# HGRN2 attention and low-rank mixer on one core: DMAs of the unused path on ScalarE, a branch hint, four first loads, and four blocks mixed as one piece

## Chip, cores, metric

The kernel runs on one core of a Trainium2 chip. The metric is the time of one launch in microseconds (us) of device time; of several runs the median is given. A profiled execution of the same program gives the trace that all other numbers come from.

## What is computed

```python
f = sigmoid(f_logit)                                  # q, k, v, f_logit: (4, 8, 768, 48)
for t in range(768):
    state = f[:, :, t, :, None] * state + k[:, :, t] (outer) v[:, :, t]
    y[:, :, t] = q[:, :, t] @ state
x = y.transpose(0, 2, 1, 3).reshape(4, 768, 384)
h = (x.transpose(0, 2, 1) @ U) @ V                    # U (768, 32), V (32, 768)
u = x + h.transpose(0, 2, 1)
out = u + relu(u @ w_ch1) @ w_ch2                     # 384 -> 1536 -> 384
```

The weights arrive in float64 and are turned into float32 on the chip; everything else is float32.

## The kernel before

Two paths are in the program. `factored_path` (L538) does the work by blocks of 64 and 128 tokens, with gates kept as sums of logarithms, and also finds out whether the gates allow this: a flag `ok` (L1304, read at L1603). `general_path` (L1309) stands inside `tc.If(good == 0)` (L1604) and computes the same in a way that holds for any gates. For the inputs here the flag is 1 and the general path is jumped over: each engine that has code in it ends with a compare-and-branch (L1604) to a target behind that code. The program's last steps (L1632) are semaphores between the engines.

**Attention.** A unit is one batch and two heads: 16 units, four in a batch. For a unit the logits are loaded by `load` (L603), on SyncE's queue, 128 tokens on the partitions in six blocks. For unit 0 they then go through `logs` in two halves of three blocks: a clamp on VectorE (L775), an exponential and a logarithm on ScalarE (L777, L779), sums over time by products on TensorE (`log_sums`, L790), and exponentials of these (L803 to L808). Keys and queries are multiplied by these, and scores (L926), states (L974), the sums of states (L996, L1000) and outputs (L1012, L1030) follow; the scans over time are on VectorE (L827, L845). TensorE's order is written out by hand for the whole kernel (`manual_schedule`); VectorE's, ScalarE's and SyncE's for the first part only. Elsewhere a scheduler orders VectorE and ScalarE, and adds of the mixer go in at high priority (`add`, L201 to L204).

Ahead of all this stands a `blank` tile, 128x384, that is set to zero (L640) and read by warm-up products (`busy`, L1131) while the first loads are under way. After the loads of unit 0's f, k and q come those of the next unit's f and unit 0's v.

**Mixer.** The class at L157 holds the steps for one batch: `low_rank` (L187) and `added_up` (L194) make h for four groups of 32 rows; `mix(t)` (L208) multiplies one 128-token block's slice of V (32 rows, in row group t modulo 4 of the array) with h, 128x384, and after every second block adds both to x in one VectorE instruction of 128x768; `turn` (L253) transposes x into uT; `ch1` (L273) and `ch2` (L324) are the two large products; `seven` (L371) does the second with seven products of half-size blocks where `sums` of weights are at hand, and `fewer` (L422) the first with fifteen products instead of eighteen, from sums of weights and of x. `store` (L318) writes 128 tokens from SyncE.

The mixer of batch b runs piece by piece between the steps of batch b+1's attention (`Fill`). Where a batch's mixing stands:

- Batch 0's is done in parts of columns by `mix_of` (L234) near 41 us; the change doesn't touch it.
- Batches 1 and 2: `start_mixer` (L1112) runs `before`: `low_rank`, `added_up`, all six `mix`, then `turn`, with the last pieces of the batch before (`after`, second products) between them.
- Batch 3, in the last stage, after all attention: the list at L1277 to L1306 puts `low[:2]` and the three pieces of `mixes` (L510; each a pair of blocks) between pieces of `fewer` of another pair of blocks; `of(i, "ready")` are sums of z on VectorE that `seven` needs.

**PSUM.** Tiles come from two pools: `ps_big`, three tiles of two banks (mixing pairs, transposes, products of `fewer`), and `ps_mm`, two tiles of one bank (`low_rank`, `ch1`'s pz, `ch2`'s po, which is filled in four quarters and so is held over other pieces). [...] A tile is given out in turn, and its next writer waits for its last reader.

**DMA.** Eight semaphores are used in turn by all DMAs: each DMA waits for the one eight before it, and at the end SyncE waits for each.

Of the kernel before, what the change touches and what calls it, by code (L numbers as in the profile page):

```python
# [10 lines left out]
F32 = mybir.dt.float32  # L11
# [4 lines left out]
ALU = mybir.AluOpType  # L16
# [43 lines left out]
def weight_loader(nc, pool, dma):  # L60

    P = nc.NUM_PARTITIONS

    def load(dst, w, place=None):
        if w.dtype == F32:  # L70
            return lambda: dma.dma_start(out=dst, in_=w), *[lambda: None] * 3
        rows, n = dst.shape[0], dst.free_size()
        T = {}

        def shaped(t):
            return t if len(dst.shape) == 2 else t.rearrange("p (c n) -> p c n", c=dst.shape[1])


        def start():
            raw = pool.tile([P, WP], U64, name="w_raw", bufs=RAW) if place is None else place()  # L80
            raw = T["raw"] = raw[0:rows, 0:n]
            dma.dma_start(out=shaped(raw), in_=w)

        def halves():
            y = pool.tile([P, WP], U32, name="w_y")[0:rows, 0:n]
            r = pool.tile([P, WP], I32, name="w_r", bufs=3)[0:rows, 0:n]
            words = T["raw"].bitcast(U32).rearrange("p (n two) -> p n two", two=2)
            lo, hi = words[:, :, 0], words[:, :, 1]

            f = y.bitcast(F32)  # L90
            nc.scalar.activation(f, hi.bitcast(F32), AF.Abs)  # L91
            nc.scalar.activation(r, lo, AF.Copy, scale=2.0**-29)
            T["parts"] = y, r, hi

        def join():
            y, r, hi = T["parts"]
            f = y.bitcast(F32)
            nc.vector.tensor_scalar(f, f, SMALLEST, LARGEST, ALU.max, ALU.min)  # L98
            nc.vector.tensor_scalar(y, y, 3, 0x3FFFFFFF, ALU.logical_shift_left, ALU.bitwise_and)
            nc.vector.scalar_tensor_tensor(y, hi, 0xC0000000, y, ALU.bitwise_and, ALU.bitwise_or)  # L100
            nc.gpsimd.tensor_tensor(dst.bitcast(I32), shaped(y.bitcast(I32)), shaped(r), ALU.add)  # L101

        def end():
            halves()
            join()

        return start, end, halves, join

    return load
# [47 lines left out]
class Mixer:  # L157
# [6 lines left out]
    def __init__(self, tc, b, x, U, V, w1, w2, sums, ident, blocks, out, two, three, zp, ps_big, ps_mm, wide=False,  # L164
                 z_all=None, room=None, pair=0):
        nc = tc.nc
# [41 lines left out]
        def mix(t):  # L208

            s = t % 2  # L210
            if s == 0:
                pu[0] = ps_big.tile([P, 2, 512], F32, name="pu", tag="big")
            g = slice((t % NG) * R, (t % NG + 1) * R)
            nc.tensor.matmul(pu[0][:, s, 0:DM], lhsT=V[g, t // NG, :], rhs=h[1][g, :], start=True, stop=True)  # L214
            if s == 1:
                add(x[:, t - 1 : t + 1, :], x[:, t - 1 : t + 1, :], pu[0][:, :, 0:DM], ALU.add)


        hs, last = {}, {}

        def low_rank_of(cols):
# [94 lines left out]
        self.some = low_rank_of, added_up_of, mix_of, turn_of, ch1_of  # L316

        def store(t, o):  # L318
            nc.sync.dma_start(out=out[b, t * P : (t + 1) * P, :], in_=o)

        po = {}
        NQ = 4
# [171 lines left out]
            return [(4 * NDC * 2 * P, lambda j=j: ch1(a, j)) for j in range(NI)]  # L494


        parts = [low_rank, added_up, lambda: [mix(t) for t in range(NCH)]]
        parts += [lambda a=a: turn(a) for a in range(NA)]
        self.before = [(DM, piece) for piece in parts]

# [6 lines left out]
            self.main += ready(a) + ahead[: NI // 2] + halved(a) + ahead[NI // 2 :]  # L507
        self.main += ready(NA - 1)
        self.after = second(NA - 1)
        self.mixes = [(DM, lambda t=t: [mix(t), mix(t + 1)]) for t in range(0, NCH, 2)]  # L510
        self.first, self.second, self.ready, self.fewer, self.halved = first, second, ready, fewer, halved
        self.sums_of_x = lambda a: [(1, lambda: sums_of_x(a))]

# [24 lines left out]
def factored_path(ctx, tc, q, k, v, f_logit, moe_U, moe_V, moe_w_ch1, moe_w_ch2, out, ok):  # L538
# [64 lines left out]
    def load(n, *names):  # L603

        b, hp = divmod(n, HP)
        for nm in names:
            if nm == "v":
                v_tiles[n] = three.tile([P, NBL, 2, D], F32, name="v_nat")
            for par in range(2):
                head = src[nm][b, 2 * hp + par]  # L610
                if nm in "kq" and n < HP:
                    if par == 0:
                        nc.sync.dma_start(
                            out=packed(n, nm).rearrange("p (h t) -> p h t", h=2),
                            in_=src[nm][b, 2 * hp : 2 * hp + 2].rearrange("h (p c) d -> p h (c d)", p=P),
                        )
                    continue
                if nm == "v" and par:

                    for s in range(2):  # L620
                        nc.sync.dma_start(
                            out=v_tiles[n][(1 - s) * C : (2 - s) * C, :, par, :],
                            in_=head.rearrange("(c s p) d -> s p c d", s=2, p=C)[s],
                        )
                    continue
                if nm == "v" or n < TURNED:
                    dst = v_tiles[n] if nm == "v" else nat[n % 2][nm]
                    nc.sync.dma_start(out=dst[:, :, par, 0:D], in_=head.rearrange("(c p) d -> p c d", p=P))
                    continue
                head = head.rearrange("(c i) d -> i c d", i=NB)  # L630
                for part in range(2):
                    p0 = par * PAD + part * NB
                    n_ch = min(NB, D - part * NB)
                    nc.sync.dma_start(  # L634
                        out=raw[n % 2][nm][p0 : p0 + NB, :].rearrange("p (c d) -> p c d", d=NB)[:, :, 0:n_ch],
                        in_=head[:, :, part * NB : part * NB + n_ch],
                    )

    blank = late[:, 5, 0 : 3 * P]
    nc.vector.memset(blank, 0.0)  # L640
    load(0, "f", "k", "q")
    load(1, "f")
    load(0, "v")

# [481 lines left out]
    with tc.manual_schedule(engines={nc.vector.engine, nc.scalar.engine}):  # L1126
# [3 lines left out]

        def busy(n, cols=DM):  # L1131
            for _ in range(n):
                nc.tensor.matmul(idle[:, 0:cols], lhsT=blank[:, 0:P], rhs=blank[:, 0:cols], start=True, stop=True)

        written = ExitStack()
        written.enter_context(tc.manual_schedule(engines={nc.sync.engine}))
# [133 lines left out]
    def of(i, kind):  # L1270
        if i >= len(pairs):
            return []
        b, a = pairs[i]
        return getattr(mixers[b], kind)(a)
# [5 lines left out]
    for i in range(len(pairs)):  # L1280
        ahead, behind = of(i + 1, "fewer"), of(i, "second")
        nxt = of(i + 2, "sums_of_x")
        if not ahead:
            todo += behind
            break
        todo += of(i, "ready")
        if i == 0:
            todo += [p for two_of in zip(ahead, low[:2] + mixers[1].mixes) for p in two_of] + behind[:1] + low[3:4] + nxt
        else:
            todo += (low[4:] if i == 1 else []) + ahead[:4] + nxt + ahead[4:5]  # L1290
            if i + 2 < len(pairs):
                todo += behind[:1]
        if i + 2 < len(pairs):
            todo += ahead[5:6] + behind[1:2] + ahead[6:7] + behind[2:3] + ahead[7:] + behind[3:]
        else:
            todo += ahead[5:6] + behind[:1] + ahead[6:] + behind[1:2] + of(i + 1, "ready") + behind[2:]
# [12 lines left out]
def general_path(ctx, tc, q, k, v, f_logit, moe_U, moe_V, moe_w_ch1, moe_w_ch2, out):  # L1309
# [87 lines left out]
    def load_unit(n):  # L1397
        b, hp = divmod(n, HP)
        for nm in "fkq":
            for par in range(2):  # L1400
                nc.sync.dma_start(
                    out=nat[n % NSLOT][nm][:, :, par, 0:D],
                    in_=src[nm][b, 2 * hp + par].rearrange("(c p) d -> p c d", p=C),
                )
        v_tiles[n] = three.tile([P, NCH, 2, D], F32, name="v_nat")
        for par in range(2):
            nc.sync.dma_start(
                out=v_tiles[n][:, :, par, :],
                in_=src["v"][b, 2 * hp + par].rearrange("(c p) d -> p c d", p=C),
            )  # L1410

    load_weight = weight_loader(nc, two, nc.sync)
    weights = [load_weight(U, moe_U.rearrange("(c p) r -> p c r", p=P))]
    weights += [load_weight(*pair) for pair in by_rows(V, moe_V, R)]
    weights += [
# [165 lines left out]
@with_exitstack  # L1581
def kernel(
    ctx: ExitStack,
    tc: tile.TileContext,
    q: bass.AP,
    k: bass.AP,
    v: bass.AP,
    f_logit: bass.AP,
    moe_U: bass.AP,
    moe_V: bass.AP,  # L1590
    moe_w_ch1: bass.AP,
    moe_w_ch2: bass.AP,
    out: bass.AP,
):


    nc = tc.nc
    args = (q, k, v, f_logit, moe_U, moe_V, moe_w_ch1, moe_w_ch2, out)
    flag = ctx.enter_context(tc.tile_pool(name="flag", bufs=1))
    ok = flag.tile([1, 1], I32, name="ok")  # L1600
    with ExitStack() as inner:
        factored_path(inner, tc, *args, ok)
    good = nc.values_load(ok[0:1, 0:1], min_val=0, max_val=1)  # L1603
    with tc.If(good == 0):  # L1604
        with ExitStack() as inner:
            general_path(inner, tc, *args)

# [29 lines left out]
```

## Time and profile before

| | |
|---|---|
| time, median of 3 runs | 471.83 us (470.58 to 473.95) |
| profiled execution, its own time | 471.81 us |
| its span (first to last instruction) | 470.0 us |
| granted TensorE clock, mean | 0.998 |
| share of the time of 16 DMA engines, 0 to 47 us | 0.80 |
| the same, 161.7 to 276 us | 0.31 |
| chain that ended last, by engine | PE 75%, DVE 13%, issue 3%, ACT 3%, DMA 2%, SyncE's queue 2% |
| costliest group | L279, 492 products 128x256, 111.5 us |

PE is TensorE, PEld its loading of weights (which overlaps PE), DVE VectorE, ACT ScalarE, POOL GpSimd, SP SyncE; a name with q (SPq, DVEq) means that engine's sequencer: register, branch, semaphore and DMA-issuing instructions. A line of a timeline gives start, length, engine, line in the kernel, operation, what it writes and reads, its shape and how many there are in the group; a bracket at the end gives idle time just before it and what ended that. A group's length contains the stops between its members. The chain of waits goes back from the last instruction to what released each one, and lists start, length and what it was. The clock stays at full speed in every slice, so lengths in different stages can be compared.

### The profile page before, as it was taken

Reading aid. Unit: us, or ns where it says so; the run is one execution under the profiler, and the core shown is the slowest. Engines: PE = TensorE matmul, PEld = TensorE weight load, DVE = VectorE, ACT = ScalarE, POOL = GpSimd, SP = SyncE. Lnnn points to the kernel's source line nnn. Section 1 sums busy time; section 2 is a strip of 40 time slices with the busy share of each in tenths; the row PEclk is TensorE's granted clock in tenths of the full one; section 3 lists DMA queues with packets and bytes.
Section 4 is the critical chain, followed back from the end, with each engine's and each line's share of the span. In section 5 each row is a group of like instructions: output and inputs, shape, how many; then the busy total and the mean of one; then the engine's idle time right before and its main releaser. Section 6 shows DMA issues by size and latency. Waiting matters only on the chain.

```text
span 470.0 us, 13005 instructions
## 1 busy us (share of the span) xinstructions
PE 456.2 (97%) x5639; PEld 394.9 (84%) x5639; DVE 352.3 (75%) x579; ACT 165.6 (35%) x315; POOL 54.2 (12%) x60
## 2 busy tenths in 40 slices
PE   7999999999999999999999999999999999999995
PEld 5876888875666578999898878989979999999995
DVE  5767788979999677775675659977796877759632
ACT  5775776562332144322323133232312312112200
POOL 2002445634112001010101001020000000000000
PEclk9999999999999999999999999999999999999999
DMA  9947997577678504506334020000000000000001
GB/s 194 209 107 191 226 220 179 155 116 106 120 120 130 83 18 52 77 7 110 48 66 73 7 52 19 12 3 20 18 1 1 35 1 35 0 16 20 1 36 40
DMA packets 148313, 34.36 MB, mean 73 GB/s; under 512 B 136790, under 2 KB 146710, under 8 KB 148246
## 3 DMA queue, kind: packets, MB, share of 16 engines
q1 hardware_dynamic: 148246, 33.44, 36.4%
q8 instruction: 46, 0.75, 0.7%
q14 instruction: 21, 0.17, 0.1%
HBM read 28.70 MB, written 4.72 MB: 71 GB/s over the span
## 4 chain that ended last, share of the span: by engine, by line
PE 75%; DVE 13%; issue 3%; ACT 3%; DMA 2%; SPq 2%; POOL 0%; DVEq 0%; ACTq 0%; POOLq 0%
PE pw L365 25%; PE pz L279 18%; PE pp L468 12%; PE po L331 5%; PE y L1012 2%; PE y L1030 2%; PE ds L974 1%; PE sc L926 1%; PE pt L744 1%; PE pt L790 1%; SPq L634 1%; PE pu L214 1%; DVE late L845 1%; DMA v_nat<-in_v_dram 1%; DVE kz L721 1%
## 5 line engine op out<-in xcount | busy, mean ns | idle before, releaser
L279 PE MATMUL pz<-uT,w 128*128 128x256 f32 x492 | 111.5, 382 | 0.3
L279 PEld LDWEIGHTS pz<-uT,w 128*128 128x128 f32 x492 | 91.7, 190 | 12.9 <-ACT uT L268 0.6
L1000 POOL COPY st<-added 128x576 f32<-128x576 f32 x12 | 18.2, 1513 | 188.0 <-DVE added L996 188.0
L365 PE MATMUL pw<-zw,w_raw 128*128 128x192 f32 x216 | 38.0, 329 | 0.0
L365 PE MATMUL pw<-w,z_all 128*128 128x192 f32 x216 | 37.3, 327 | 0.0
L101 POOL TENSOR_TENSOR w<-w_y,w_r 128x384 int32<-128x384 int32 x24 | 31.5, 1313 | 39.5 <-DVE w_y L100 23.2
L365 PEld LDWEIGHTS pw<-w,z_all 128*128 128x128 f32 x216 | 35.3, 190 | 0.5
L365 PEld LDWEIGHTS pw<-zw,w_raw 128*128 128x128 f32 x216 | 35.1, 190 | 0.6 <-issue 0.3
L314 ACT ACTIVATE z_all<-pz 128x512 f32<-128x512 f32 x33 | 19.6, 598 | 45.1 <-PE pz L279 44.6
L827 DVE TENSOR_TENSOR_SCAN late<-fz,late 128x768 f32<-128x768 f32 x12 | 21.1, 1756 | 7.3 <-ACT fz L822 7.1
L461 ACT ACTIVATE other<-other 128x512 f32<-128x512 f32 x18 | 11.3, 631 | 40.3 <-DVE other L204 40.3
L331 PE MATMUL po<-w,zw 128*128 128x384 f32 x72 | 25.2, 495 | 0.0
L331 PE MATMUL po<-w,z_all 128*128 128x384 f32 x72 | 24.7, 493 | 0.0
L939 DVE TENSOR_TENSOR A<-sc,causal 128x768 f32<-128x768 f32 x16 | 15.2, 952 | 9.5 <-PE sc L926 9.5
L845 DVE TENSOR_TENSOR_SCAN late<-fz,other 128x768 f32<-128x768 f32 x12 | 22.0, 1834 | 0.2
L331 PEld LDWEIGHTS po<-w,zw 128*128 128x128 f32 x72 | 13.2, 190 | 9.6 <-issue 0.8
L331 PEld LDWEIGHTS po<-w,z_all 128*128 128x128 f32 x72 | 13.3, 190 | 8.9 <-DVE o L204 0.6
L981 ACT COPY added<-ds 48x576 f32<-48x576 f32 (+1 forms) x28 | 17.8, 635 | 5.1 <-PE ds L974 4.7
L461 ACT ACTIVATE z_all<-z_all 128x512 f32<-128x512 f32 x12 | 7.6, 630 | 33.3 <-DVE z_all L204 33.3
L468 PE MATMUL pp<-v_nat,late 128*128 128x128 f32 x152 | 19.1, 275 | 0.0
L1012 PEld LDWEIGHTS y<-st,qT 48*64 48x64 f32 x704 | 13.6, 137 | 6.4 <-issue 3.9
L98 DVE TENSOR_SCALAR w_y<-w_y 128x384 f32<-128x384 f32 (+3 forms) x27 | 12.1, 448 | 8.9 <-ACT w_y L91 8.9
(224 smaller groups left out, 867.3 us busy)
## 6 DMA issues: line engine op xcount, KB each, us to landing
w_raw<-in_moe_w_ch_dram SPq DMA_DIRECT2D x18, 384.0 KB, 4.1
out_dram<-o SPq DMA_DIRECT2D x24, 192.0 KB, 2.0
v_nat<-in_v_dram SPq DMA_DIRECT2D x16, 144.0 KB, 4.3
v_nat<-in_v_dram SPq DMA_DIRECT2D x32, 72.0 KB, 3.9
zw<-in_moe_w_ch_dram SPq DMA_DIRECT2D x6, 384.0 KB, 5.1
w<-in_k_dram SPq DMA_DIRECT2D x4, 288.0 KB, 3.7
w<-in_q_dram SPq DMA_DIRECT2D x4, 288.0 KB, 5.1
late<-in_f_logit_dram SPq DMA_DIRECT2D x10, 96.0 KB, 3.0
```

The costliest lines, as they stand in the source:

```text
L101: nc.gpsimd.tensor_tensor(dst.bitcast(I32), shaped(y.bitcast(I32)), shaped(r), ALU.add)
L279: nc.tensor.matmul(pm[:, i * 2 * P : (i + 1) * 2 * P], lhsT=w1[:, m, o : o + P], rhs=uT[a][:, m, :], start=(m == 0), stop=(m == NDC - 1))
L314: nc.scalar.activation(z[a, c][:, k : k + 2, :].rearrange("p i t -> p (i t)"), pm, AF.Relu)
L331: nc.tensor.matmul(pm, lhsT=z[a, i // NI][:, i % NI, s * P : (s + 1) * P], rhs=w2[:, i, :], start=(i == 0), stop=(i == NFC - 1))
L365: nc.tensor.matmul(W["pm"][:, n * HM : (n + 1) * HM], lhsT=lhs[:, i, :], rhs=rhs[:, i, :], start=(i == 0), stop=(i == NI - 1))
L461: nc.scalar.activation(dst, dst, AF.Relu, scale=float(SIGNS[n]))
L468: nc.tensor.matmul(pm[:, i, r * P : (r + 1) * P], lhsT=room["w"](wn)[:, r * P : (r + 1) * P], rhs=x_node(a, xn), start=((xn, wn) == of[0]) ...
L827: nc.vector.tensor_tensor_scan(backwards(X, S - 1, S), backwards(f, S, S), backwards(ends, S - 1, S), 0.0, ALU.mult, ALU.add,)
L845: nc.vector.tensor_tensor_scan(Y, f[:, 0:S], starts, 0.0, ALU.mult, ALU.add)
L981: nc.scalar.copy(added[r, 1:].rearrange("p (e c s) -> p e c s", c=NBL, s=2), ds[r, :, 0 : NBL * D].rearrange("p s (c e) -> p e c s", e=D),)
L1000: nc.gpsimd.tensor_copy(st, states.rearrange(by_e, c=NCH))
L1012: nc.tensor.matmul(o(c % 2, par, c // 2), lhsT=T["q"][rows[par], chunk[c]], rhs=T["st"][rows[par], c, :], start=(c <= 2), stop=False, skip ...
```

## The change

1. **General path.** Its loads of q, k, v, f and of weights, and its stores, are issued by ScalarE, where SyncE issued them. None of this runs here; it changes how many instructions of each engine lie behind the branch.
2. **Hint.** A hint "likely taken" for VectorE's branch is placed, and the `If` gets the label that it names.
3. **First loads.** Unit 0's f is loaded in four pieces (blocks 0 to 2 of both heads, then blocks 3 to 5), one head on SyncE's queue and one on ScalarE's, where it was two loads of a head each on SyncE's. `blank` becomes 128x1, read with a step of 0.
4. **Mixing.** `mix_four` does blocks 0 to 3 as one piece: four products, blocks 0 and 1 into one `ps_big` tile, 2 and 3 into two `ps_mm` tiles; one add of 128x768 and two of 128x384. Blocks 4 and 5 stay a pair. It is used for batches with `sums` (1 to 3). In the last stage there are two pieces of `mixes` in place of three, and the `ready` sums of the first pair move behind the piece `ahead[4]`.

```diff
+        def mix_product(dst, t):
+            g = slice((t % NG) * R, (t % NG + 1) * R)
+            nc.tensor.matmul(dst, lhsT=V[g, t // NG, :], rhs=h[1][g, :], start=True, stop=True)
+
+        def mix_four():
+            big = ps_big.tile([P, 2, 512], F32, name="pu", tag="big")
+            pms = [big[:, s, :] for s in range(2)] + [ps_mm.tile([P, 512], F32, name="pu1", tag="mm") for _ in range(2)]
+            for t, pm in enumerate(pms):
+                mix_product(pm[:, 0:DM], t)
+            add(x[:, 0:2, :], x[:, 0:2, :], big[:, :, 0:DM], ALU.add)
+            for t in range(2, NG):
+                add(x[:, t, :], x[:, t, :], pms[t][:, 0:DM], ALU.add)
+
+        def mix_blocks():
+            first = 0
+            if sums is not None:
+                mix_four()
+                first = NG
+            for t in range(first, NCH):
+                mix(t)
...
         def store(t, o):
-            nc.sync.dma_start(out=out[b, t * P : (t + 1) * P, :], in_=o)
+            by = nc.scalar if z_all is None else nc.sync
+            by.dma_start(out=out[b, t * P : (t + 1) * P, :], in_=o)
...
-        parts = [low_rank, added_up, lambda: [mix(t) for t in range(NCH)]]
+        parts = [low_rank, added_up, mix_blocks]
...
-        self.mixes = [(DM, lambda t=t: [mix(t), mix(t + 1)]) for t in range(0, NCH, 2)]
+        self.mixes = [(DM, mix_four), (DM, lambda: [mix(t) for t in range(NG, NCH)])]
...
-    blank = late[:, 5, 0 : 3 * P]
+    blank = late[:, 5, 0:1]
     nc.vector.memset(blank, 0.0)
-    load(0, "f", "k", "q")
+    queues = nc.sync, nc.scalar
+    for m in range(2):
+        some = slice(m * NBL // 2, (m + 1) * NBL // 2)
+        for par in range(2):
+            queues[par].dma_start(out=nat[0]["f"][:, some, par, 0:D],
+                                  in_=f_logit[0, par].rearrange("(c p) d -> p c d", p=P)[:, some, :])
+    load(0, "k", "q")
     load(1, "f")
     load(0, "v")
...
-                nc.tensor.matmul(idle[:, 0:cols], lhsT=blank[:, 0:P], rhs=blank[:, 0:cols], start=True, stop=True)
+                nc.tensor.matmul(idle[:, 0:cols], lhsT=blank.broadcast_to((P, P)), rhs=blank.broadcast_to((P, cols)),
+                                 start=True, stop=True)
...
-        todo += of(i, "ready")
         if i == 0:
-            todo += [p for two_of in zip(ahead, low[:2] + mixers[1].mixes) for p in two_of] + behind[:1] + low[3:4] + nxt
+            todo += [p for two_of in zip(ahead, low[:2] + mixers[1].mixes) for p in two_of] + ahead[4:5]
+            todo += of(0, "ready") + behind[:1] + low[3:4] + nxt
         else:
-            todo += (low[4:] if i == 1 else []) + ahead[:4] + nxt + ahead[4:5]
+            todo += of(i, "ready") + (low[4:] if i == 1 else []) + ahead[:4] + nxt + ahead[4:5]
...
-            nc.sync.dma_start(
+            nc.scalar.dma_start(
                     out=nat[n % NSLOT][nm][:, :, par, 0:D],
...
-    load_weight = weight_loader(nc, two, nc.sync)
+    load_weight = weight_loader(nc, two, nc.scalar)
...
+    tc.mark_branch_hint_location("general", "LikelyTaken", engines=[nc.vector.engine])
     good = nc.values_load(ok[0:1, 0:1], min_val=0, max_val=1)
-    with tc.If(good == 0):
+    with tc.If(good == 0, label="general"):
```

More of the change, by code (lines that the diff above doesn't have):

```diff
@@ L1406, in load_unit @@
         for par in range(2):
-            nc.sync.dma_start(
+            nc.scalar.dma_start(
                 out=v_tiles[n][:, :, par, :],
```

## Prediction

> **What bounds the kernel now.** I read the page's first part, then the windows view by stage, then the chain of waits at the start, and the timelines of TensorE and VectorE around the code that changes.
>
> ```profile
> PE 456.2 (97%) x5639; PEld 394.9 (84%) x5639; DVE 352.3 (75%) x579; ACT 165.6 (35%) x315; POOL 54.2 (12%) x60
> ```
> ```profile
> 161.70:276.00 114.30, 114.00 (x1384) 100.44 (x1382) 79.37 (x108) 34.25 (x62) 4.85 (x4) 1.00 0.31 51
> ```
> TensorE is busy 456.2 of 470.0 us. In the second line (stage, length, then busy time of PE, PEld, DVE, ACT, POOL) it lacks only 0.3 us of 114.3. So an edit counts by what it adds to or takes from TensorE's idle time; only the first microseconds, before TensorE has data, and the last ones, after its last product, belong to others. The start, from the chain of waits (start, length, what):
>
> ```profile
> 0.81 0.45 SPq L628
> ...
> 1.32 3.39 DMA late<-in_f_logit_dram
> ...
> 4.81 0.32 DVE late L775
> ...
> 5.16 0.45 ACT late L777
> ...
> 5.63 0.45 ACT late L779
> ...
> 6.17 1.71 PE pt L790 x12
> ```
> The two loads of unit 0's gates, issued at 0.81 and 1.32, take 2.8 and 3.4 us (least and most of "DMA to landing" of these two): landings at about 3.65 and 4.71. The clamp L775 waits for the second.
>
> The mixing of batch 1 (first two lines TensorE's timeline, last two VectorE's):
>
> ```profile
> 160.17 1.56 PE L214 MATMUL pu<-h,V 32*128 32x384 f32 x12
> 161.66 4.14 PE L331 MATMUL po<-w,zw 128*128 128x384 f32 x12
> ```
> ```profile
> 160.18 1.76 DVE L845 TENSOR_TENSOR_SCAN late<-fz,other 128x768 f32<-128x768 f32 x1
> 161.85 2.66 DVE L204 TENSOR_TENSOR x<-x,pu 128x768 f32<-128x768 f32 x3
> ```
> TensorE goes through twelve passes (six blocks) in 1.49 us without a stop, while VectorE is still in a scan. Then batch 2's and the last batch's mixing on TensorE:
>
> ```profile
> 270.70 1.99 PE L214 MATMUL pu<-h,V 32*128 32x384 f32 x12
> 272.67 2.22 PE L365 MATMUL pw<-w,w_raw 128*128 128x192 f32 x12
> ```
> ```profile
> 342.02 0.92 PE L214 MATMUL pu<-h,V 32*128 32x384 f32 x4
> 343.38 1.13 PE L468 MATMUL pp<-st,fz 128*128 128x128 f32 x8 [0.44 <-DVE qT L204]
> 344.34 1.06 PE L468 MATMUL pp<-uT,late 128*128 128x128 f32 x8
> 345.95 0.91 PE L214 MATMUL pu<-h,V 32*128 32x384 f32 x4 [0.55 <-DVE x L204]
> ...
> 348.78 0.91 PE L214 MATMUL pu<-h,V 32*128 32x384 f32 x4
> 349.62 4.17 PE L365 MATMUL pw<-w,other 128*128 128x192 f32 x24
> ```
> And the branch at the end (its instructions by engine, with duration in ns and start):
>
> ```profile
> L1604 SPq EVENT_SEMAPHORE  x8: 17/17/17, 468.1 to 468.6; - x8
> ...
> L1604 DVEq COMPARE_BRANCH  x1: 72/72/72, 465.3 to 465.3; - x1
> L1604 SPq COMPARE_BRANCH  x1: 50/50/50, 465.4 to 465.4; - x1
> ...
> L1604 DVEq EVENT_SEMAPHORE  x1: 21/21/21, 468.5 to 468.5; - x1
> ```
> SyncE jumps at 465.4 and shows its next instruction 2.6 us later; VectorE's jump takes 3.1 us. The last store is issued at 465.03 and lands 2.0 later, at 467.06: both jumps end after it, so they hold the end.
>
> [...]
>
> **The change, part by part.**
>
> *First gate loads.* Four loads of half size on two queues, both halves of blocks 0–2 first: issued near 0.8 on SyncE and ScalarE at once. The bytes are the same and all gate loads finish together near 4.4 to 4.7; the first halves, issued as early as before's first load, should land near its 3.65 or earlier. Then the clamp runs at 3.75 (0.32), exp 4.07 (0.45), log 4.53 (0.45), and TensorE can start at 5.05. The second half follows: clamp end about 5.1, exp 5.5 (ScalarE is busy until then), log end near 6.0. So the L790 products (1.71) end about 6.88, before 7.88: 1.0 us, or 0.7 if the second half lands at 5.0. Two more issues on ScalarE come ahead of its table load (1.28 us), which then ends near 3.2, under the 4.07 where it is needed. SyncE still issues two loads before k and q, and v lands at 9.1 to 10.1 for a need at 10.6. The smaller memset (0.38 to some 0.06 us) starts the warm-up products earlier, so these don't hold TensorE at 5.05. From here the chain has only SyncE waits tied to work that moves along; I take 0.9, ends 0 (the DMA share before 47 us is 0.80, so k, q and v may come no earlier) and 1.1.
>
> *Mixing of batch 1.* Blocks 0 and 1 get a two-bank tile, 2 and 3 a single bank each. At 160 one of the two single banks holds a half-done po (L331). So block 3 must wait until VectorE's add has read block 2, and VectorE comes to this only after the scan (161.85) and the add of blocks 0 and 1 (pitch 0.87): 162.72 + 0.55 for a 128x384 add = 163.27. TensorE then has three products left, 0.84 us (the x4 row at 342.02 took 0.85 to its follower): po starts at 164.17 instead of 161.66, +2.5. Behind the waiting product stands all of TensorE, and for it wait VectorE's o<-x,po (165.83) and the turn into uT on ScalarE. As the stage has 0.3 us of idle time, nothing gives this back. Ends: 0, if the po bank is free there, and 3.5, if the scheduler's order on VectorE puts another piece between.
>
> *Mixing of batch 2.* Here no single bank is held; before, the third pair had to wait for a double one, until VectorE was done with pw (271.63). After, six blocks fit without a wait: 1.49 instead of 1.97, -0.5 (0 to -0.5).
>
> *Mixing of the last batch.* Before, three pairs at 342.02, 345.95, 348.78, each 0.84 for two blocks: the passes of a pair use two row groups of 32. Four blocks fill four row groups and should take the 0.84 of one pair; the third pair's 0.84 goes. The order gives VectorE qT<-A,pp earlier too, since a 0.95 sum (w<-other,w, at 341.68) moves behind: the 0.44 wait and most of the 0.55 go. Added: pp from 342.87, two groups 1.99 to 344.86, pair 4+5 at 345.07 (it waits for the x add, 0.2), pp to 347.89, where pw started at 349.62: -1.7 (ends -0.8, if the four run one after the other, and -1.9). The extra add (two of 0.55 instead of one 0.95) is hidden under VectorE's waits of 1.3 to 1.9 us at 354 to 366; without these it costs 0.15.
>
> *General path.* It isn't run, but its code lies between each branch and its target. In the built program SyncE's share falls from 287 instructions to 1, and ScalarE's rises from 371 to 585. [...]it next waits for the landing at 467.06, not 468.08: -1.0 from SyncE. ScalarE jumps at 455.4, 10 us before the end[...]. VectorE's 652 instructions keep their 3.1 us, and its semaphore at 468.48 gates the program's last steps (0.5 us before what SyncE needs at 469.0)[...]. The hint is one instruction, built in as VectorE's very first. No trace shows one. If it works -1.0 in all; if not -0.5. I take -1.0; ends 0 and -1.0, and +3.1 for the rival below.
>
> Sum: -0.9 + 2.5 - 0.5 - 1.7 - 1.0 = -1.6 on a span of 470.0, so 468.4, and 470.2 with the 1.8 outside it (profiled execution 471.81, median 471.83: no correction).
>
> **Rivals.** (a) *Most gains don't arrive*: the hint does nothing (-0.5 only), and the 0.9 at the start is lost again to the loads of 10 to 47 us. Then -0.5 + 2.5 - 0.5 - 1.7 = -0.2: 471.6. For it: a DMA share of 0.80; against: the first loads of each later step have slack of 2.6 us. (b) *The stall of batch 1 isn't there*, because the scheduler puts the adds ahead of the scan or the bank is free: -4.1, 467.7. Against it: adds wait on TensorE's products at 160.2, just when the scan starts. (c) [...] (the other side): it sits before VectorE's first memset[...]. I price it at VectorE's jump, 3.1 us; its memsets (0.96 to 3.6) would then push the clamp, due at 3.75, past 6. -1.6 + 0.5 + 3.1 = +2.0: 473.8. It decides from 1.6 us on. For it: nothing else stands so early[...].
>
> **How the numbers follow.** Likeliest 0.48: 470.2 (own range 469.0 to 471.3). (a) 0.19, (b) 0.14, (c) 0.14, others 0.05. 80% from 467.5 to 473.4: it takes in (a), most of (b) and the lower part of (c). One per cent, 4.7 us, is about what a measurement can tell from no change. Faster than 467.1 needs (b) and more: 0.05. Slower than 476.5 needs (c) with a second loss: 0.06. The rest 0.89.
>
> **What would show it.** Right: the first clamp near 3.75 and L790 done near 6.9; one gap of 2.3 to 2.5 us on TensorE before the fourth mixing product near 161, released by VectorE's x; none in the mixing near 270; pw in the last stage 1.7 earlier relative to 338; SyncE's first L1604 event with the landing; VectorE's under 0.5 us after its branch. Wrong: a VectorE that starts late, or a gap near 161 that is absent or over 3.5 us.

## The result, and the profile after

The changed kernel takes 472.66 us (median of 22 runs, 469.39 to 475.04), the kernel before beside it 472.45 (22 runs, 470.29 to 474.59): ratio 1.0007, 95% interval 0.999 to 1.0024. The forecast of 470.2 was 0.34% below before; the interval excludes that. The medians of the kernel before differ a little between comparisons (471.75 to 472.47), so ratios count below.

The profiled execution took 475.04 us (span 473.2), the longest of the 22. That turns out to be useful, since it shows two things that I had not counted. In the lines below pu is the tile of the mixing's products, po that of `ch2`, pw that of `seven`, and put that of the transposes into uT. First the page's line of busy time, then the windows view around batch 1's mixing (stage, length, busy PE, PEld, DVE, ACT, POOL, granted clock, DMA share, GB/s):

```profile
PE 459.4 (97%) x5639; PEld 397.2 (84%) x5639; DVE 352.4 (74%) x582; ACT 166.0 (35%) x315; POOL 54.4 (11%) x60
```
```profile
163.70:165.90 2.20, 0.00 (x0) 0.00 (x0) 2.15 (x3) 0.00 (x0) 0.00 (x0) 1.00 0.00 0
167.10:170.40 3.30, 3.30 (x6) 1.67 (x5) 1.17 (x2) 0.00 (x0) 0.00 (x0) 0.50 0.00 0
170.50:174.00 3.50, 3.35 (x44) 2.14 (x42) 1.38 (x2) 0.85 (x2) 0.00 (x0) 1.00 0.00 0
```
TensorE does as many products as before, but is 3.2 us longer busy. It stands still for 2.2 us, and soon after that runs for 3.3 us at a granted clock of 0.50: six passes of po that start 0.64 us apart, where at full clock they start 0.32 apart. That is time that the busy column counts as work.

The stop itself, on TensorE and on VectorE (timelines of the changed kernel):

```profile
162.77 0.92 PE L221 MATMUL pu<-h,V 32*128 32x384 f32 x6
165.91 0.58 PE L221 MATMUL pu<-h,V 32*128 32x384 f32 x1 [2.21 <-DVE x L204]
```
```profile
162.78 1.76 DVE L873 TENSOR_TENSOR_SCAN late<-fz,other 128x768 f32<-128x768 f32 x1
164.46 1.39 DVE L204 TENSOR_TENSOR x<-x,pu 128x768 f32<-128x768 f32 x2
```
Three blocks go through, and the fourth waits for VectorE's adds behind the scan. (The trace names both adds in one row; the second has 128x384.) This is the wait that was forecast.

Batch 2, and the last stage up to pw, on TensorE:

```profile
277.48 0.93 PE L221 MATMUL pu<-h,V 32*128 32x384 f32 x8
278.23 0.81 PE L214 MATMUL pu<-h,V 32*128 32x384 f32 x4
278.96 2.22 PE L387 MATMUL pw<-w,w_raw 128*128 128x192 f32 x12
```
```profile
348.31 0.93 PE L221 MATMUL pu<-h,V 32*128 32x384 f32 x8
...
351.37 0.91 PE L214 MATMUL pu<-h,V 32*128 32x384 f32 x4 [0.15 <-DVE x L204]
...
354.10 2.12 PE L387 MATMUL pw<-w,other 128*128 128x192 f32 x12
```
Eight passes of four blocks take as long as four passes of two did (0.93 against 0.92), and in batch 2 the mixing takes 1.48 us from its first pass to pw, where it took 1.97.

The start, from the chain of waits, and the branch (durations in ns, then starts):

```profile
1.07 4.21 PE idle L1161 x6
...
5.31 2.23 PE pt L818 x12
```
```profile
L1634 SPq EVENT_SEMAPHORE  x8: 17/17/17, 471.3 to 471.8; - x8
...
L1634 DVEq COMPARE_BRANCH  x1: 84/84/84, 469.7 to 469.7; - x1
...
L1634 DVEq EVENT_SEMAPHORE  x1: 21/21/21, 470.3 to 470.3; - x1
```
L818 is L790 of before. It starts 0.86 us earlier, but takes 2.23 us in place of 1.71. At the end VectorE's jump takes 0.6 us, not 3.2, and SyncE's first semaphore (471.30) follows the last store's landing (471.29).

If each TensorE instruction is matched with its twin in the trace of before, the changed kernel lags behind by this much (us; a minus means that it is ahead):

| place | lag |
|---|---|
| end of L790 | -0.33 |
| 31 us, after two stops without a semaphore (before has one there) | +1.57 |
| 37 us, after a first stretch of half clock (34.0 to 37.4) | +2.76 |
| first pass of batch 1's mixing | +2.60 |
| po behind it | +5.10 |
| end of the second stretch of half clock | +6.79 |
| pw after batch 2's mixing | +6.30 |
| pw in the last stage | +4.48 |
| last product | +4.38 |
| end, with 3.84 us after VectorE's last add in place of 4.99 | +3.23 |

### The profile page after: what moved, and what is told of

It is laid out like the page before. It is cut to its first block, busy times and chain, and to the rows that moved or that the text cites. A ratio compares the mean times of both kernels' runs of the same rounds, so it can differ in the third digit from the quotient of the medians.

```text
span 473.2 us, 13013 instructions
## 1 busy us (share of the span) xinstructions
PE 459.4 (97%) x5639; PEld 397.2 (84%) x5639; DVE 352.4 (74%) x582; ACT 166.0 (35%) x315; POOL 54.4 (11%) x60
## 4 chain that ended last, share of the span: by engine, by line
PE 77%; DVE 12%; issue 3%; ACT 3%; DMA 3%; SPq 1%; POOL 0%; DVEq 0%; ACTq 0%; POOLq 0%
PE pw L387 25%; PE pz L300 20%; PE pp L490 12%; PE po L353 4%; PE y L1040 2%; PE y L1058 2%; DMA v_nat<-in_v_dram 2%; PE sc L954 2%; PE pt L772 2%; PE pt L818 1%; PE ds L1002 1%; DVE late L873 1%; DVE late L855 1%; PE pt L981 1%; DVE late L908 1%
## 5 line engine op out<-in xcount | busy, mean ns | idle before, releaser
L353 PE MATMUL po<-w,zw 128*128 128x384 f32 x72 | 26.8, 521 | 0.0
```

The source lines that it names most:

```text
L353: nc.tensor.matmul(pm, lhsT=z[a, i // NI][:, i % NI, s * P : (s + 1) * P], rhs=w2[:, i, :], start=(i == 0), stop=(i == NFC - 1))
```

## Experiments

**One part each, and batch 1 undone.** Four kernels on one chip, with 43 runs of the kernel before (median 471.75).

*pairs_batch1*: the changed kernel, where batch 1 goes without the piece of four.

```diff
-            if sums is not None:
+            if sums is not None and b != 1:
                 mix_four()
```


> The changed kernel, but batch 1's six blocks are mixed as three pairs, as before; batches 2 and 3 keep the piece of four. Theory (stall and clock): in the changed kernel's profiled execution TensorE stood 2.2 us before the fourth product and then had half its clock for 3.4 us (167.1 to 170.5), together 4.0 us from one matched product to the next. Both must be gone: the pu passes in about 1.5 us without a gap, no half clock between 160 and 175, and the median 2 to 4 us below the changed kernel's 472.7, so 469 to 470.5, some 0.5% under the kernel before. Rival (the stall is made up for later): the gap goes, the time stays within 1 us of 472.5.

468.51 us, ratio 0.9931 (0.9917 to 0.9945). The pu passes take 1.49 us without a stop, and none of its six executions is under a mean clock of 0.998. One line of the change costs 3.6 us against the changed kernel (ratios 1.0007 and 0.9931: 0.76%), more than the 2.5 of the wait (+2.60 to +5.10 above). At 0.69% under the kernel before it is also faster than the 0.5% that was expected.

*head_only*: before with the four loads and the small blank; *tail_only*: before with the general path's DMAs moved and the hint; *mix_only*: before with the mixing and its order in the last stage. Each is that part of the diff, alone.

> The kernel before with the four first loads and the 128x1 blank alone. Theory[...]: L790 is done 0.3 to 1.0 us before the 7.98 of the kernel before, 0.3 where the clock becomes full only after 5.5 us; between 20 and 40 us the stops that wait for no semaphore, 0.98 us before and 2.6 after, come at the same instructions, 256 apart, of a length that changes from execution to execution; median within 0.7 us of the kernel before. Rival (as forecast): 0.9 is kept to the end. Rival (the change of the loads itself delays later loads): the lead turns into a loss of over 1 us that waits for a DMA show.

471.99 us, 1.0004 (0.999 to 1.0019). In its profile L790 is done at 7.01, against 7.87 before, yet the median shows no gain.

> The kernel before with the general path's DMAs on ScalarE and the hint alone. Theory: from VectorE's last add to the end 3.8 us instead of 5.0, so 1.2 less, about 471.2; VectorE's jump about 0.5 us instead of 3.1, SyncE's next instruction within 0.05 of the last store's landing. Rival (the hint costs something at the start): TensorE's first products of L790 start later than 6.2, and the gain is less than 0.5. Its head and its mixing are those of the kernel before: its list of clocks shows how often that has a stretch of half clock; theory: rarely, and none at 160 to 175.

470.51 us, 0.9975 (0.9963 to 0.9986): -1.2. From VectorE's last add to the end 3.62 us, where the profile of before has 4.99.

> The kernel before with the mixing of four blocks alone, for batches 1 to 3, and the order of the last stage that goes with it. Theory: +2.2 to +4.0 at batch 1 (the wait, and the half clock where it follows), -0.3 at batch 2, -2.0 in the last stage: 0 to +1.7, so 472.4 to 474. Rival (the wait is hidden): -2.3, 470.1. Rival (last stage gains nothing): +2 to +4.

472.96 us, 1.0032 (1.0012 to 1.0051): +1.5. Its 17 executions fall into groups by mean clock: 472.04 (median of 6, clock 0.997 and more), 474.03 (5, clock 0.994 to 0.996), 475.51 (6, under 0.994). None of the 43 executions of before is under 0.994. The three parts add up to 0.2 - 1.2 + 1.5 = +0.5, about the +0.3 of the whole.

**Is it the stop that brings the half clock?** *stall_warm* keeps the wait and gives TensorE something to do in it:

```diff
             for t, pm in enumerate(pms):
+                if t == 3 and b == 1:
+                    spare = ps_big.tile([P, 2, 512], F32, name="spare", tag="big")
+                    for _ in range(3):
+                        nc.tensor.matmul(spare[:, 0, 0:DM], lhsT=ident, rhs=h[1], start=True, stop=True)
                 mix_product(pm[:, 0:DM], t)
```


> The changed kernel with three extra products (identity by h, 128x384, result unused) between batch 1's third and fourth mixing product, where TensorE stood for 2.2 us. They fill about 1.9 us of it. Theory (the stop costs twice, by itself and by the half clock that follows): po starts where it did, within 0.3 us, but no half clock follows, so executions under a mean clock of 0.994 vanish; median 0.8 to 1.8 us below the changed kernel's 472.66, so about 471.3. Rival (the half clock has another reason, or costs nothing): clocks and time as in the changed kernel, or later by what the extra products take beyond the gap.

471.37 us, 0.9988 (0.9976 to 1.0). TensorE's timeline:

```profile
161.70 2.20 PE L230 MATMUL spare<-h,ident 128*128 128x384 f32 x6
...
164.83 4.14 PE L357 MATMUL po<-w,zw 128*128 128x384 f32 x12
```
po starts 3.98 us after the first pu (160.85), as in the changed kernel (162.77 to 166.76, 3.99), and its twelve passes take the usual 4.14 us. 19 of 22 executions have a mean clock of 0.997 or more, where the changed kernel had 4 of 22; one is under 0.994, where it had 8. Doing useless work in the gap takes 1.3 us off the median. So the half clock is the stop's second price: it goes when the stop is filled, and it goes when the stop is taken away (pairs_batch1).

**The tail in its parts.** *tail_no_hint* has the moved DMAs only, *hint_only* the hint only.

> The kernel before with the general path's DMAs on ScalarE, without the hint. Theory: VectorE's jump takes 3.1 us again and its semaphore comes 3.2 us after its branch, where SyncE waits for it: from VectorE's last add to the end about 4.4 us, 0.5 us less than the 5.0 of the kernel before and 0.6 more than with the hint; median about 471.2. Rival (VectorE's jump doesn't matter): 3.8 us as with the hint.

471.54 us, 0.9988 (0.9972 to 1.0003); tail 4.42 us, as worked out. At the branch's line SyncE is early and VectorE late:

```profile
L1605 SPq EVENT_SEMAPHORE  x8: 17/17/17, 464.7 to 466.1; - x8
...
L1605 DVEq EVENT_SEMAPHORE  x1: 21/21/21, 467.5 to 467.5; - x1
```


> The kernel before with the hint alone; the general path's DMAs stay on SyncE. Theory: VectorE's jump 0.5 us, but SyncE's jump still takes 2.6 us, so from VectorE's last add to the end about 5.0 us as in the kernel before, median within 0.4 of it; TensorE's first products start as in the kernel before, so the hint costs nothing. Rival[...]: L790 starts later than 6.3 us, and the median is 1 to 3 us up.

472.95 us, 1.0016 (1.0 to 1.0032); tail 5.16 us: VectorE is ready 0.6 us after its branch, but SyncE's jump takes 2.83, so the end gains nothing. L790 starts at 5.90, among the profiles with the old loads (5.74 to 6.73), and the hint takes 0.05 us on VectorE, so rival (c) has nothing in the trace. The median is 0.8 us over the kernel before, where at most 0.4 was expected. That lies at the edge of the interval; I can't attribute it.

**The stops without a semaphore.** In the changed kernel TensorE stands twice for over a microsecond near 25 and 30 us without any semaphore to wait for:

```profile
26.82 0.49 PE L1058 MATMUL y<-v_nat,A 64*64 64x48 f32 x18 [1.35 <-issue]
...
29.54 0.92 PE L954 MATMUL sc<-qT,kz 48*64 48x64 f32 x46
31.72 0.27 PE L954 MATMUL sc<-qT,kz 48*64 48x64 f32 x2 [1.26 <-issue]
```
Before them stand 961 and 1217 recorded instructions of TensorE, 256 apart. In all 18 profiles every such stop of over 0.15 us from 12 us on stands behind 705, 961, 1217, 1473 or 1985 of them, always a multiple of 256 apart. The profile's page shows on queue q8 46 transfers of kind "instruction", 0.75 MB, so 16 KB each, beside 11278 product and weight instructions of TensorE, 245 to a transfer. One runs from 24.49 to 25.44 us and one from 29.42 to 30.43, each ending 0.03 us before one of these stops begins (25.47 and 30.46). That such a transfer brings a stretch of TensorE's code is an estimate from these counts, and that the stops have to do with it isn't shown. *shift_blocks* moves the count against the program (on the kernel with batch 1 in pairs):

```diff
-        busy(3)
+        busy(1)
+        busy(8, 16)
```


> The changed kernel with batch 1 mixed in pairs, and a warm-up of one large and eight small products (16 columns) in place of three large ones: TensorE has 24 product and weight instructions more ahead of unit 0. Theory[...]: the stops come after the same number of recorded TensorE instructions as before, about 962 and 1218, so 12 products earlier in the program: in the group y<-v_nat,A after some 16 products and not after 28. Rival (they belong to the data of that product): the same products, 986 and 1242 instructions. The time is not the question; it may be up to 1 us later, since the warm-up ends later and TensorE's clock may be full later.

```profile
29.82 0.79 PE L954 MATMUL sc<-qT,kz 48*64 48x64 f32 x34
32.13 0.46 PE L954 MATMUL sc<-qT,kz 48*64 48x64 f32 x14 [1.52 <-issue]
```
The stop comes again after 1217 instructions, and so twelve passes earlier in the group (34 and 14 in place of 46 and 2). The stops belong to the count of instructions, not to the product's data. (470.51 us, 0.9966, 0.9951 to 0.9982: by the ratios 1.7 us over pairs_batch1. In its profile the clock is full only at 11.2 us, which may be why; it was not tested.)

Whether the stops come from the data traffic was tried by holding two weight loads back (*later_weights*). `elif n == 2:` allots the tile, writes one column of it from x and issues the two loads, which at n == 1 are left out:

> The changed kernel with batch 1 in pairs, and the first two loads of w_ch1 (384 KB each, issued near 25 us while all DMA engines are busy) held back to about 31 us, where the DMA engines stood idle. Theory[...]:[...] the stop at instruction 1217 (0 to 1.5 us in nine profiles) is under 0.3, and the median is 0.3 to 1 us lower than without. Rival (the stops have nothing to do with data traffic): same stop, same time. What can spoil it: the weights come too late near 42 us, which a wait of ScalarE or VectorE for w_raw would show.

468.25 us, 0.9907 (0.9877 to 0.9937), beside 468.18 for the same kernel without (*pairs_again*). No stop at 1217, but two of 0.30 and 0.25 before it; and four profiles with the loads in their place (pairs_batch1, pairs_old_head, tail_no_hint, last_stage_only) have none at 1217 either, so this run settles nothing. Traffic alone is not it: in the trace of before the windows view gives a DMA share of 1.03 from 47 to 71 us, more than the 0.80 from 20 to 30, and no such stop comes. But from 47 to 71 TensorE goes through 11 product and weight instructions in a us, and from 20 to 30 through 56. After 36 us the 18 profiles have one such stop (four_on_sync, 0.45 us at 45.7). Whether the pace of the instructions, the traffic or both bring the stops stays open.

**What the four loads are worth.** On the kernel with batch 1 in pairs, with and without them, twice.

> The changed kernel with batch 1 mixed in pairs once more, as the base of the two runs beside it. Theory: 0.6 to 0.8% under the kernel before, as in its first run (0.9931); no execution under a mean clock of 0.994.

468.18 us, 0.9911 (0.9875 to 0.9946).

> The changed kernel with batch 1 in pairs, and with the head of the kernel before: unit 0's f in two loads on SyncE, blank of 128x384. Theory (the four loads are worth about 0.2 us[...]): median within 0.7 us of the same kernel with four loads. Rival (as forecast): 0.9 us or more above it.

467.37 us, 0.9903 (0.9867 to 0.9939).

> As in its first run: batch 1 in pairs, tail and last stage changed, head of the kernel before. Theory (the four loads gain about 0.5 us at L790[...]): L790 done at 7.4 to 8.4, stops in sum 0 to 1, and a median within 0.5 us of the same kernel with four loads. Rival (the four loads cost): it stays 0.8 us or more below, as in the first comparison (467.37 against 468.18).

468.38 us, 0.993 (0.9905 to 0.9954).

> The same with four first loads and the 128x1 blank. Theory: L790 done at 7.0 to 7.6, stops in sum 0.3 to 2.6, first put<-ident,x near 42 to 43 as without. Rival (they cost): 0.8 us or more slower than with the old head.

468.87 us, 0.9927 (0.9907 to 0.9948). All runs of each kind together: with the four loads 468.49 (18 runs), without 467.91 (13 runs); means 468.59 and 468.47. There is no gain, and the runs can't tell a cost from none.

> The four loads all on SyncE's queue, one after the other. Theory: the second halves are issued near 1.8 and 2.3 and all later loads 1 us later, so L790 is done near 7.5 to 8.0, and the time is 0 to 1 us over that of the two queues. Rival (ScalarE's queue itself costs something): it is faster than with two queues by 0.5 or more.

468.88 us, 0.9923 (0.9906 to 0.9941): the second queue makes no difference.

> The head of the kernel before with the 128x1 blank alone. Theory: the warm-up starts 0.3 us earlier, the loads land as before: same time as the old head, within 0.5 us. Rival (the broadcast operands or the earlier warm-up cost): 0.5 us or more above it.

468.72 us, 0.9929 (0.9909 to 0.9949): nor does the blank.

The profiles tell where the lead goes (us; the stops are those without a semaphore from 12 to 36 us, summed; an asterisk marks a stretch of half clock before 42 us, and its row is left out of the last mean; kernels with another edit ahead of 42 us are left out):

| two loads | L790 done | stops | first put, batch 0 | four loads | L790 done | stops | first put |
|---|---|---|---|---|---|---|---|
| before | 7.87 | 0.98 | 42.99 | after | 7.54 | 2.61 | 45.55* |
| tail_only | 7.52 | 1.95 | 43.72 | pairs_batch1 | 7.49 | 0.37 | 42.01 |
| mix_only | 7.44 | 0.33 | 41.90 | head_only | 7.01 | 0.69 | 42.07 |
| tail_no_hint | 7.48 | 0 | 41.80 | stall_warm | 7.18 | 2.09 | 43.63 |
| hint_only | 8.23 | 1.42 | 44.99* | pairs_again | 7.59 | 0.89 | 42.66 |
| last_stage_only | 8.43 | 0 | 42.62 | four_again | 7.03 | 1.81 | 43.20 |
| pairs_old_head | 7.90 | 0 | 41.86 | | | | |
| old_head_again | 7.59 | 1.19 | 43.14 | | | | |
| mean | 7.81 | 0.73 | 42.58 (7) | | 7.31 | 1.41 | 42.71 (5) |

The four loads bring L790 forward by 0.5 us; the stops are 0.7 longer; at 42 us nothing is left. That the stops take back what TensorE has gained fits this, but with stops from 0 to 1.95 us with two loads and from 0.37 to 2.61 with four it is argued, not shown.

At the other end the four loads cost something that the traces do show. SyncE's waits at the branch's line, in four_again and in old_head_again:

```profile
L1634 SPq EVENT_SEMAPHORE  x8: 17/17/17, 464.7 to 465.3; - x8
```
```profile
L1627 SPq EVENT_SEMAPHORE  x8: 17/17/17, 463.4 to 464.8; - x8
```
The last store lands at 464.73 and 464.72, but the spans are 466.7 and 466.2. The eight DMA semaphores are used in turn, so two more loads shift the last store's from the seventh of SyncE's eight waits to the first. All the other waits then come after the landing, where six used to be done before it. In all eight profiles with four first loads, the moved DMAs and the hint it takes 1.93 us from the landing to the end; in the four with two loads, 1.46. Where SyncE's jump is long this doesn't show: head_only has 2.83, and before 2.93.

**The last stage by itself.** *last_stage_only* has `mix_four` in `mixes` and the new order; batches 1 and 2 stay in pairs.

> The kernel before with the last batch's mixing as a piece of four and a pair, and with the order of the last stage that goes with it; batches 1 and 2 as before. Theory: -1.9 (from 338 to pw near 350, as in three profiles), so 0.4% less, and no half clock that the kernel before does not have. Rival (what is gained before 350 is lost in the waits for VectorE behind it): within 0.5 us of the kernel before.

470.64 us, 0.9963 (0.9946 to 0.998): -1.7, so what is won before 350 us is kept.

## Why the prediction was wrong

Point by point:

- **Batch 1's mixing, +2.5.** The mechanism, the place and the releaser were as forecast, the stop 2.21 us, and the way from the first pass to po 3.99 us in place of 1.49: +2.50. What failed is the term itself, "+2.5" as the whole price, with its upper end of 3.5 given to VectorE's order and the clock put at nothing. After the stop TensorE's clock is halved for one stretch of 3.41 us in the profiled execution (1.7 us lost) and for 6.83 us in that of mix_only, where this begins 0.34 us before the stop ends. The mean clocks say that most executions have such a stretch (18 of 22 are under 0.997, against 8 of 43 of before). All in all the piece of four costs 3.6 us here by the ratios. Within a trace these stretches begin at whole multiples of 3.413 us after the first record of full clock: that is at 6.65 us in the changed kernel, and the stretches begin at 33.96 and 167.07, 8 and 47 multiples later; at 4.90 in mix_only, and the stretch begins at 161.91, 46 later. So a stop may lie between two of these multiples in one execution and across one in the next. That this is why not every execution loses clock is an estimate from these times, and was not tested. I had called the clock a constant because every slice of the page of before shows 9, 90% or more.
- **First gate loads, -0.9.** The first clamp started at 3.70 (forecast 3.75), so the loads do what was said. The term was mis-sized in four places. The base was one execution with its first clamp at 4.81; eight other profiles with the old loads have 4.38 to 5.37, on average 4.63, so some 0.2 of the "1.0 us" was chance. L790 met half the clock: its first passes came every 0.21 us, the last six every 0.11, so it ended at 7.54, not 6.88. (The trace's first record of full clock is at 6.65 us, in the middle of L790; in that of before it is at 4.25, ahead of it. Lengths at the start can't be compared as if the clock were the same.) And "from here the chain has only SyncE waits tied to work that moves along" overlooked the 0.98 us of "issue" at 29.2 that the chain of before already showed: a stop behind 1217 instructions, without a semaphore, and no wait that moves along. And at the end the shifted semaphores cost 0.47 us, which was put at nothing. Measured: 0.5 at L790, no gain at the end.
- **Batch 2, -0.5.** -0.49 in the trace. Right.
- **Last batch, -1.7.** -1.8 in the trace, -1.7 by last_stage_only's ratio. Right: four blocks in four row groups took 0.93 us, one pair in two 0.92.
- **General path and hint, -1.0.** -1.15 in the trace, -1.2 by tail_only's ratio. That SyncE's jump would shorten was an estimate, with no such jump in a trace yet: in tail_only its next instruction comes 0.2 us after its branch (466.5 to 466.7), where it came 2.6 us after it before. Both halves are needed, as forecast: 4.42 us without the hint, 5.16 with it alone, 3.62 with both. From the last store's landing to the end it is 2.93 before, 1.93 in the changed kernel and 1.46 in tail_only, so with the old loads this part alone is worth more than the 1.0.
- **The sum.** With +3.6 for batch 1 and 0 for the loads: 3.6 - 0.5 - 1.8 - 1.2 = +0.1, against the measured +0.3. The two terms that failed were off by 1.1 (batch 1) and 0.9 (first loads), and the forecast was 1.9 too low.
- **The rivals.** Half of (a) came true, since the gain at the start was lost, though no later load is shown to have taken it: the clock in L790, the stops without a semaphore and the order of the last waits stand in its place. (b) and (c) did not come true.

The best version found is the changed kernel with batch 1 in pairs: 0.7 to 1.0% under the kernel before in all its forms but the one with the smaller warm-up, with four loads or with two.

## What to carry to other kernels

The stop of TensorE is priced twice here: by its length (2.21 us), and by the half clock that can follow it (3.41 us in the profiled execution); before taking a wait like this one of 2.2 us on a full TensorE, look for work to put into it, or for a buffer. The borrowed single buffers were only free where no one held one of them, so the same edit gained 0.49 us in batch 2 and cost 2.50 in batch 1 before the half clock is counted. Where semaphores are used in turn, two loads more at the start can move the last store's wait at the end (0.47 us here), so read the end too. And a gain of under a microsecond in a start where the same product starts 1 us earlier or later from one execution to the next needs more than one profile as its base.

## What was not expected of the hardware

- A hint that stands ahead of VectorE's first memset, some 740 recorded instructions ahead of its branch, still shortens the jump from 3.1–3.2 to 0.6 us (before and tail_no_hint; after and hint_only), and costs 0.05 us where it stands.
- Stretches of half clock of 3.41 us, or twice that, after stops of 2.2 us (batch 1), and also after stops of 1.3 to 1.4 us among small products (after, at 34 us, and hint_only, at 31), though not after one of 1.2 us in tail_only.
- TensorE stops of up to 1.5 us (1.52 in shift_blocks) at instructions a multiple of 256 apart, where it goes through some 56 product and weight instructions in a us, of another length in each execution.
